# One transfer queue becomes two: GpSimd issues the later loads, the second readings and the output of an attention and feed-forward kernel

## The chip, the cores and the metric

The kernel runs on one core of one Trainium2 chip. The metric is the device time of one execution in microseconds (us). It was taken three times for the kernel before: 593.48, 593.84 and 595.53 us, with 593.84 us as the median. One further execution was recorded by the hardware profiler; that one took 598.99 us, of which 597.2 us lie between its first and its last instruction (the span).

## What is computed

Attention over 4 sequences of 768 tokens with 8 heads of 64, in which a query sees the last 96 keys and the first 8 keys of its sequence, with a bias that falls with the distance; then a feed-forward network on all 3072 rows. Cut from the reference:

```python
# q, k, v: (4, 8, 768, 64); n_global = 8; n_local = 96
scores = np.matmul(q, k.transpose(0, 1, 3, 2)) / np.sqrt(D)
keep = is_global | is_local          # first 8 keys, or 0 <= row - column < 96
bias = -slopes * dist                # slopes: 2 ** -(head + 1)
a = softmax(np.where(keep, scores + bias, -1e9))
x = np.matmul(a, v)                  # to (3072, 512)
h = x @ w_in                         # (512, 2048)
g = h / (1.0 + np.exp(-1.702 * h))
out = g @ w_out                      # (2048, 512), fp32
```

## The kernel before

**Tiles.** The 24 blocks are 128 rows each: blocks 0 to 3 are the first blocks of the four sequences, blocks 4 to 23 the rest in order. Because of the window, a later block needs its own keys and values and those of the block before it, and the first rows of its sequence. Two blocks make a chunk of the feed-forward part, 12 chunks in all. fp32 values are split into two fp16 halves, and each product is the sum of three fp16 products; from chunk 3 on the first matrix product is done in seven quarter products instead of eight (`up_two`, tiles pa and pb).

**What a later block passes through.** Its q, k and v are loaded into a tile raw (`load`, L406; two such tiles in turn, 256 KB for each of the three). ScalarE and VectorE split them (L464, L465, L474, L475). A transposing transfer brings q and k into QK (L467), and two plain transfers make a copy of the keys in QK with the halves exchanged (L469). Then in four units of two heads: scores on TensorE (L545, tile s), row minimum on VectorE (L551), exponential on ScalarE (L561), the split into halves (L565, L566, tile hl), a transposing transfer (L567, from hl to pt), and the products with the values on TensorE (L576 to L578, tile pv). The first rows' values, kept in VG, are written into rows of the block's own VR by a small transfer (`leading`, L668) when the block's own products are done; the next block's products read them there. For the first block after a sequence's first, k and v of that one are loaded again (`handover`, L507, tile over). The result is normalised (L694), split (L716, L718) and transposed by a transfer (L719) into xT, the input of the feed-forward part.

**The second readings.** To check that the fast path is exact enough, q, k and v of blocks 0 to 3 (L1011, tile again) and all weights in halves (L1019, tiles ws_..again, 32 transfers of 512 KB) are read a second time, squared and summed on ScalarE (L413, L1021) and reduced on VectorE (L1023). A flag made from these decides at the end if a slow general path runs; with the given inputs it does not.

**The order.** Every operation is a task with the engines that may run it, an assumed duration, its predecessors, its buffers and a due date. `order` (L109) passes the due dates backwards, adds a number out of the table NUDGE by the task's tag (L129), and then plays the tasks through in assumed time: each engine takes the most urgent task that is ready. The order that comes out is the program order of every engine, fixed when the program is built; on the chip each engine goes through its row in that order and waits at each instruction for what that one needs. SyncE ("SP") is one of these engines and issues all transfers but three; a transfer that waits, or one that takes long to issue, holds up all those behind it in SP's row. GpSimd (POOL) writes a few constants at the start and has nothing to do after that.

Of the kernel before, what the change touches and what calls it, by code (L numbers as in the profile page):

```python
# [19 lines left out]
P = 128  # L20
# [9 lines left out]
NUDGE = {"T3": 12.3, "block0": -11.9, "block13": -0.8, "block2": -18.8, "block4": 7.7, "block7": -8.8,  # L30
# [12 lines left out]
EARLY = 4  # L43
# [6 lines left out]
BACKLOG = 3.0  # L50
TWO = 3
LAT = 0.2
# [40 lines left out]
class Work:  # L93
# [15 lines left out]
    def order(self):  # L109
# [10 lines left out]
        while moved:  # L120
            moved = False
            for t in reversed(self.tasks):
                for n in t.next + [b.ring.line[b.i + b.ring.bufs].users[0] for b in t.bufs
                                   if not b.ring.loose and b.i + b.ring.bufs < len(b.ring.line)]:
                    due = n.due - min(n.on.values()) - LAT - (2.5 if "SP" in t.on else 0.0)
                    if due < t.due:
                        t.due, moved = due, True
        for t in self.tasks:
            t.due += NUDGE.get(t.tag, 0.0)  # L129
        free = dict.fromkeys(("PE", "DVE", "ACT", "POOL", "SP"), 0.0)  # L130
        dma, now, done = 1.5, 0.0, []
# [3 lines left out]
        while len(done) < len(self.tasks) + spared:  # L135
            moved = False
            for e in free:
                if free[e] > now or (e == "SP" and dma > now + BACKLOG):
                    continue
# [36 lines left out]
                if e == "SP":  # L176
                    free[e] = now + 0.1
                    dma = max(dma, now + 1.95) + us
                    t.end = dma + 0.9
# [15 lines left out]
            if not moved:  # L195
                later = [x + 1e-6 for x in (t.early() for t in ready) if x > now]
                later += [x for x in (*free.values(), dma - BACKLOG + 1e-6) if x > now] + [at for at in ready.values() if at > now]
# [6 lines left out]
def load_weights(nc, ws, w_in, w_out, s, u, half=None):  # L204
# [6 lines left out]
    nc.sync.dma_start(ws.rearrange("p (c f) t -> p c (f t)", c=n), words.rearrange("(c p) f -> p c f", p=P))  # L211
# [3 lines left out]
def kernel(  # L215
# [22 lines left out]
    ENG = {"PE": nc.tensor, "DVE": nc.vector, "ACT": nc.scalar, "POOL": nc.gpsimd, "SP": nc.sync}  # L238
# [123 lines left out]
    def weights(s, u):  # L362
# [8 lines left out]
        t0 = add({"SP": 2.75}, lambda e: load_weights(nc, ws(), w_in, w_out, s, u), bufs=[ws])  # L371
# [32 lines left out]
    def load(n, raw, parts=(0, 1, 2)):  # L404
        b, i = place(n)
        return [add({"SP": 1.35}, lambda e, z=z: nc.sync.dma_start(  # L406
# [93 lines left out]
    def handover(n):  # L500
# [6 lines left out]
        ld = load(b, raw, (1, 2))  # L507
# [395 lines left out]
    def pile(c, t, g, ready, part, steps, want):  # L903
# [15 lines left out]
        for k_, y in enumerate(ys[c][t]):  # L919
# [4 lines left out]
            if end:  # L924
# [7 lines left out]
                add({"ACT": 0.6} if last else {"SP": 0.7 * w / DM}, lambda e, m=m: ENG[e].dma_start(  # L932
# [76 lines left out]
    for n in range(EARLY):  # L1009
        raw = Buf(r_raw, [P, 3, H, D], F32, f"again{n}")  # L1010
        ld = load(n, raw)  # L1011
# [3 lines left out]
    for s in range(NST):  # L1015
        for u in range(2):
            for half in range(2):
                ws = Buf(r_wa, [P, 512, 2], I32, f"ws{s}_{u}{half}again")
                t0 = add({"SP": 1.6}, lambda e, s=s, u=u, ws=ws, half=half: load_weights(nc, ws(), w_in, w_out, s, u, half), bufs=[ws])  # L1019
# [266 lines left out]
```

## Time and profile before

| | |
|---|---|
| median of three runs | 593.84 us |
| profiled execution, its own time | 598.99 us |
| span in that execution | 597.2 us |
| TensorE busy, share of the span | 578.5 us, 97% |
| VectorE busy | 496.0 us, 83% |
| ScalarE busy | 463.6 us, 78% |
| GpSimd busy | 5.8 us, 1% |
| bytes moved by transfers | 109.58 MB |

Busy time is the time in which an engine executes an instruction; issuing a transfer does not count, so SyncE has no busy time here. Names: PE is TensorE, PEld its loading of weights, DVE VectorE, ACT ScalarE, POOL GpSimd, SP SyncE, and SPq the queue of SyncE, whose rows are the issuing of transfers. A row of groups gives line, engine, operation, tiles, shapes and count, then the busy us and the mean ns of one, then the idle time of the engine just before. L406 is line 406 of the kernel before; in the changed kernel the lines stand 8 or 9 lower (L406 is L415, L211 is L219, L932 is L941, L567 is L576, L668 is L677).

### The profile page before, as it was taken

The page shows a single profiled execution, that of the slowest core. Times are in us where ns is not written, and L with a number is a line of the kernel's source. Part 1 is how long each engine was busy: PE and PEld are TensorE (multiplying, and loading weights), DVE is VectorE, ACT ScalarE, POOL GpSimd, SP SyncE. Part 2 cuts the span into 40 slices and gives each one's busy share as a digit, 9 for nine tenths or more (in the row PEclk, how much of TensorE's full clock was granted, in tenths as well). Part 3 has the DMA queues.
Part 4 walks back from the last instruction along what each step waited for, and adds up shares of the span by engine and source line. Part 5 has one row for each costly group of instructions (what it writes and reads, how often), then busy time and mean ns, then how long its engine had stood idle before and what let it go on. Part 6 is the DMA issues. An engine that isn't in the chain of part 4 may idle for free.

```text
span 597.2 us, 16877 instructions
## 1 busy us (share of the span) xinstructions
PE 578.5 (97%) x6741; PEld 435.2 (73%) x6742; DVE 496.0 (83%) x1167; ACT 463.6 (78%) x1092; POOL 5.8 (1%) x18
## 2 busy tenths in 40 slices
PE   7999999999999999999999999899999999999996
PEld 4887576777668778868677768667777667777895
DVE  6799899999999999987798798798788878785541
ACT  4888699898948878978687999778988878844432
POOL 3000000000000000000000000000000000000000
PEclk9999999999999999999999999999999999999999
DMA  8999999999987579969999999999979999930001
GB/s 223 311 301 251 275 230 247 187 213 168 193 167 125 102 134 191 152 144 215 212 182 198 224 218 208 209 225 203 237 154 203 221 222 227 220 67 1 36 2 41
DMA packets 268503, 109.58 MB, mean 183 GB/s; under 512 B 249537, under 2 KB 250049, under 8 KB 268417
## 3 DMA queue, kind: packets, MB, share of 16 engines
q1 hardware_dynamic: 267984, 108.30, 90.0%
q8 instruction: 54, 0.88, 0.6%
q14 instruction: 33, 0.26, 0.2%
q10 hardware_dynamic: 432, 0.13, 0.1%
HBM read 57.67 MB, written 6.29 MB: 107 GB/s over the span
## 4 chain that ended last, share of the span: by engine, by line
PE 73%; DMA 14%; DVE 6%; ACT 3%; issue 2%; SPq 1%; ACTq 0%; DVEq 0%
PE y L914 31%; PE pa L846 12%; PE pb L846 9%; PE h L806 8%; DMA pt<-hl 6%; PE s L545 4%; DMA QKover<-QKover 2%; PE pv L576 1%; PE sT L638 1%; PE pv L578 1%; PE pv L577 1%; DMA QKover<-qk16over 1%; DMA VR<-VG 1%; DMA again<-in_k_dram 1%; DVE hl L566 1%
## 5 line engine op out<-in xcount | busy, mean ns | idle before, releaser
L914 PE MATMUL y<-w,g 128*128 128x512 f16 (+1 forms) x1248 | 264.6, 363 | 0.8 <-DVE w L381 0.5
L914 PEld LDWEIGHTS <-g 128*128 128x128 f16 x1248 | 118.2, 98 | 107.3 <-DVE g L818 1.4
L846 PEld LDWEIGHTS <-w 128*128 128x128 f16 x1728 | 100.5, 98 | 4.5 <-DVE h L854 0.9
L561 ACT ACTIVATE p<-p,NM 128x232 f32<-128x232 f32 x160 | 76.6, 481 | 10.5 <-DVE NM L551 10.2
L846 PEld LDWEIGHTS <-T 128*128 128x128 f16 x1296 | 76.8, 98 | 4.6
L806 PE MATMUL h<-xT,w 128*128 128x256 f16 x576 | 67.1, 273 | 0.0
L551 DVE CUSTOM_DVE_ANT_0 p<-s,mm 128x232 f32<-128x232 f32 x160 | 57.3, 393 | 7.6 <-PE s L545 7.3
L806 PEld LDWEIGHTS <-w 128*128 128x128 f16 x576 | 55.6, 98 | 8.1
L566 DVE TENSOR_TENSOR hl<-p,hl 128x464 f16<-128x464 f32 x80 | 50.9, 636 | 11.6 <-ACT hl L565 11.1
L887 DVE SCALAR_TENSOR_TENSOR g<-t,g 128x512 f16<-128x512 f32 x72 | 49.2, 686 | 10.2 <-ACT g L886 9.6
L886 ACT ACTIVATE g<-t 128x512 f16<-128x512 f32 x72 | 44.9, 626 | 13.1 <-DVE t L879 11.9
L565 ACT CAST hl<-p 128x464 f16<-128x464 f32 x80 | 46.1, 576 | 3.1 <-DMA pt<-hl 1.3
L878 ACT ACTIVATE t<-h 128x512 f32<-128x512 f32 (+1 forms) x72 | 35.5, 515 | 16.1 <-DVE h L854 14.8
L846 PE MATMUL pa<-xS,T 128*128 128x128 f16 x648 | 45.0, 219 | 0.0
L879 DVE SCALAR_TENSOR_TENSOR t<-t,h 128x512 f32<-128x512 f32 (+1 forms) x72 | 38.4, 552 | 7.5 <-ACT t L878 7.4
L854 DVE TENSOR_TENSOR h<-pb,h 128x256 f32<-128x256 f32 x72 | 28.6, 417 | 19.3 <-PE pb L846 16.9
L545 PEld LDWEIGHTS <-QK 128*128 128x128 f16 x640 | 36.2, 98 | 5.1 <-DVE NM L551 1.7
L846 PE MATMUL pb<-xS,w 128*128 128x128 f16 x540 | 37.5, 219 | 1.0 <-DVE h L854 0.9
L545 PE MATMUL s<-QK 128*128 128x128 f16 x320 | 38.3, 219 | 0.0
L576 PE MATMUL pv<-VR,pt 128*128 128x64 f16 x288 | 34.6, 193 | 3.6 <-DMA VR<-VG 2.3
L846 PE MATMUL pa<-xT,w 128*128 128x128 f16 x540 | 37.3, 219 | 0.0
L576 PEld LDWEIGHTS <-pt 128*128 128x128 f16 x320 | 29.5, 98 | 10.2 <-DMA pt<-hl 4.0
(179 smaller groups left out, 1033.0 us busy)
## 6 DMA issues: line engine op xcount, KB each, us to landing
ws<-in_moe_w_in_dram SPq DMA_DIRECT2D x8, 1024.0 KB
ws<-in_moe_w_out_dram SPq DMA_DIRECT2D x8, 1024.0 KB
raw<-in_q_dram SPq DMA_DIRECT2D x24, 256.0 KB
raw<-in_k_dram SPq DMA_DIRECT2D x24, 256.0 KB
out_dram<-yo SPq DMA_DIRECT2D x22, 256.0 KB
raw<-in_v_dram SPq DMA_DIRECT2D x20, 256.0 KB
QK<-QK SPq DMA_DIRECT2D x40, 128.0 KB
ws_00again<-in_moe_w_in_dram SPq DMA_DIRECT2D x8, 512.0 KB
```

The costliest lines, as they stand in the source:

```text
L545: nc.tensor.matmul(sp()[:, j, lo:hi], d["QK"]()[:, 0, h, :], K[:, 1 + z, h, P - (hi - lo):], start=(z == 0), stop=(z == 1), skip_group_che ...
L551: nc.vector.tensor_tensor_reduce(out=pr()[:, j, :], in0=sp()[:, j, :], in1=m, scale=-1.0 / SC, scalar=3.0e38, op0=ALU.add, op1=ALU.min, ac ...
L561: ex.append(add({"ACT": 0.473}, lambda e, j=j: nc.scalar.activation(pr()[:, j, :], pr()[:, j, :], AF.Exp, bias=NM[:, n, hs[j]:hs[j] + 1], ...
L565: t4 = add({"ACT": 0.5}, lambda e: nc.scalar.copy(hl()[:, 0, :, SKIP:], pr()), ex, [pr, hl])
L566: t5 = add({"DVE": 0.55}, lambda e: nc.vector.tensor_sub(hl()[:, 1, :, SKIP:], pr(), hl()[:, 0, :, SKIP:]), [t4], [pr, hl])
L576: nc.tensor.matmul(o, ph, V[:, 0, h], start=(s == 0), stop=False, skip_group_check=True)
L806: nc.tensor.matmul(ph()[:, fi, :], w1(s, cc, z, fi), X[:, y, cc, :], start=(j + cc == 0), stop=(j == 2 and cc == NCC - 1))
L846: nc.tensor.matmul(o()[:, fi], w, x()[:, y * NCC + 2 * k + cc, t], start=(first and fi + j + cc == 0), stop=(last and j + cc == 3), skip_g ...
L879: return add({"DVE": 0.08 + 0.265 * w}, lambda e: nc.vector.scalar_tensor_tensor(o(), o(), 1.0, src(), ALU.add, ALU.mult), [t1], srcs)
L886: t4 = add({"ACT": 0.53}, lambda e, g=g, tt=tt: nc.scalar.mul(g()[:, 0], tt(), SG / (SX * SW)), u, [tt, g])
L887: t5 = add({"DVE": 0.61}, lambda e, g=g, tt=tt: nc.vector.scalar_tensor_tensor(g()[:, 1], tt(), SG / (SX * SW), g()[:, 0], ALU.mult, ALU.s ...
L914: nc.tensor.matmul(y(), part(zg, f), w2(s, z, f % 2)[:, m], start=(begin and f + j == 0), stop=(end and j == 2 and f == 2 * len(steps) - 1 ...
```

## The change

A second engine name for issuing transfers, "GP", is added to the planner. It is GpSimd's queue, with a row of its own, costs of its own, and its own assumed state of the transfers under way. These tasks move to it: the loads of q, k and v from block 4 on, the loads of `handover`, the second readings of q, k, v and of the weights, and the output of all chunks but the last. On SP stay the loads of blocks 0 to 3, the first reading of the weights, the transposing transfers, the copies inside the core's memory, and the output of the last chunk (one of its pieces on ScalarE, as before). The table NUDGE is replaced as a whole.

```diff
-NUDGE = {"T3": 12.3, "block0": -11.9, "block13": -0.8, "block2": -18.8, "block4": 7.7, "block7": -8.8,
...
+NUDGE = {"": -3.9, "T2": 1.5, "block0": -39.8, "block10": 2.9, "block12": 0.8, "block14": -15.4,
...
-                    due = n.due - min(n.on.values()) - LAT - (2.5 if "SP" in t.on else 0.0)
+                    due = n.due - min(n.on.values()) - LAT - (2.5 if "SP" in t.on else 3.5 if "GP" in t.on else 0.0)
...
-        free = dict.fromkeys(("PE", "DVE", "ACT", "POOL", "SP"), 0.0)
-        dma, now, done = 1.5, 0.0, []
+        free = dict.fromkeys(("PE", "DVE", "ACT", "POOL", "SP", "GP"), 0.0)
+        dma, now, done = {"SP": 1.5, "GP": 1.5}, 0.0, []
...
-                if free[e] > now or (e == "SP" and dma > now + BACKLOG):
+                if free[e] > now or (e in dma and dma[e] > now + BACKLOG):
...
-                if e == "SP":
-                    free[e] = now + 0.1
-                    dma = max(dma, now + 1.95) + us
-                    t.end = dma + 0.9
+                if e in dma:
+                    free[e] = now + (0.1 if e == "SP" else 1.2)
+                    dma[e] = max(dma[e], now + (1.95 if e == "SP" else 2.8)) + us
+                    t.end = dma[e] + 0.9
...
-    ENG = {"PE": nc.tensor, "DVE": nc.vector, "ACT": nc.scalar, "POOL": nc.gpsimd, "SP": nc.sync}
+    ENG = {"PE": nc.tensor, "DVE": nc.vector, "ACT": nc.scalar, "POOL": nc.gpsimd, "SP": nc.sync, "GP": nc.gpsimd}
...
-    def load(n, raw, parts=(0, 1, 2)):
+    def load(n, raw, parts=(0, 1, 2), late=False):
         b, i = place(n)
-        return [add({"SP": 1.35}, lambda e, z=z: nc.sync.dma_start(
+        on = "SP" if n < EARLY and not late else "GP"
+        return [add({on: 1.35}, lambda e, z=z: ENG[e].dma_start(
...
-        ld = load(b, raw, (1, 2))
+        ld = load(b, raw, (1, 2), True)
...
-                add({"ACT": 0.6} if last else {"SP": 0.7 * w / DM}, lambda e, m=m: ENG[e].dma_start(
+                add({"ACT": 0.6} if last else {"SP" if c == NCHUNK - 1 else "GP": 0.7 * w / DM}, lambda e, m=m: ENG[e].dma_start(
...
-        ld = load(n, raw)
+        ld = load(n, raw, late=True)
...
-                t0 = add({"SP": 1.6}, lambda e, s=s, u=u, ws=ws, half=half: load_weights(nc, ws(), w_in, w_out, s, u, half), bufs=[ws])
+                t0 = add({"GP": 1.6}, lambda e, s=s, u=u, ws=ws, half=half: load_weights(ENG[e], ws(), w_in, w_out, s, u, half), bufs=[ws])
```

The numbers in these lines are the planner's assumptions; nothing on the chip reads them. What they change is the order. In all, 134 transfers go from SP's row to POOL's: 60 loads of raw, 8 of over, 12 of again, 32 halves of weights and 22 pieces of output.

The first place is where the products of block 17 read the first rows' values that were put into VR16. SP's row before, from the last transpose of block 16 on (names: pt16_3 is unit 3 of block 16, over19 the repeated keys and values before block 19, ws2_11again a half of the second reading, yo6_0 a piece of output):

```order
L567 DMA_TRANSPOSE pt16_3_6012<-hl1_90 128x8x128
L469 DMA QK18_5897<-QK18_5897 64x1024 x2
L406 DMA over19_6074<-in_k_dram 128x8x64
L567 DMA_TRANSPOSE pt17_0_6133<-hl0_89 128x8x128
L211 DMA ws3_00again_6151<-in_moe_w_in_dram 128x2x512
L567 DMA_TRANSPOSE pt17_1_6180<-hl1_90 128x8x128
L406 DMA over19_6074<-in_v_dram 128x8x64
L668 DMA VR16_5075<-VG2_4995 8x1024
L932 DMA out_0_dram<-yo6_0_6210 128x512
```

SP's row in the changed kernel, from the same transpose on:

```order
L576 DMA_TRANSPOSE pt16_3_5921<-hl1_90 128x8x128
L478 DMA QK18_5881<-QK18_5881 64x1024 x2
L677 DMA VR16_5014<-VG2_4411 8x1024
L576 DMA_TRANSPOSE pt17_0_6129<-hl0_89 128x8x128
L576 DMA_TRANSPOSE pt17_1_6182<-hl1_90 128x8x128
L728 DMA_TRANSPOSE xT8_6191<-x1616_6184 128x8x128
```

And POOL's row in the changed kernel, where the transfers that left that place now stand:

```order
L219 DMA ws3_00again_6127<-in_moe_w_in_dram 128x2x512
L941 DMA out_0_dram<-yo6_0_6162 128x512
L415 DMA over19_6187<-in_k_dram 128x8x64
L941 DMA out_0_dram<-yo6_1_6206 128x512
L219 DMA ws3_01again_6282<-in_moe_w_in_dram 128x2x512
L415 DMA raw20_6336<-in_q_dram 128x8x64
L415 DMA raw20_6336<-in_k_dram 128x8x64
L219 DMA ws3_10again_6390<-in_moe_w_out_dram 128x1024
L415 DMA over19_6187<-in_v_dram 128x8x64
```

Before, five transfers stand between the copy of keys and that of VR16, three of them loads; now none does, the two transposes come behind it, and the loads have a row of their own, in which they wait only for one another's buffers and for the output tiles.

The second place is three blocks earlier, at the units of block 14. SP's row before, from unit 0 on (VG2 takes the first rows' values out of VRover14):

```order
L567 DMA_TRANSPOSE pt14_0_4871<-hl0_89 128x8x128
L567 DMA_TRANSPOSE pt14_1_4918<-hl1_90 128x8x128
L406 DMA raw16_4793<-in_v_dram 128x8x64
L567 DMA_TRANSPOSE pt14_2_4992<-hl0_89 128x8x128
L487 DMA VG2_4995<-VRover14_4787 8x1024
L211 DMA ws1_00again_5054<-in_moe_w_in_dram 128x2x512
L211 DMA ws1_01again_5071<-in_moe_w_in_dram 128x2x512
L567 DMA_TRANSPOSE pt14_3_5078<-hl1_90 128x8x128
```

SP's row in the changed kernel, from unit 2 of that block on:

```order
L576 DMA_TRANSPOSE pt14_2_5117<-hl0_89 128x8x128
L576 DMA_TRANSPOSE pt14_3_5173<-hl1_90 128x8x128
L576 DMA_TRANSPOSE pt15_0_5220<-hl0_89 128x8x128
L476 DMA_TRANSPOSE QK16_5303<-qk1616_0_4932 128x16x128
L576 DMA_TRANSPOSE pt15_1_5354<-hl1_90 128x8x128
```

The two halves of weights of 512 KB each, which stood right ahead of the transpose of unit 3, are gone from the row, and transposes follow one another.

More of the change, by code (lines that the diff above doesn't have):

```diff
@@ L196, in order @@
                 later = [x + 1e-6 for x in (t.early() for t in ready) if x > now]
-                later += [x for x in (*free.values(), dma - BACKLOG + 1e-6) if x > now] + [at for at in ready.values() if at > now]
+                later += [x for x in (*free.values(), *(x - BACKLOG + 1e-6 for x in dma.values())) if x > now] + [at for at in ready.values() if at > now]
                 later += [x for t in done[-64:] for x in (t.end, t.end + LAT) if x > now] + ([worked + GAP + 1e-6] if now < worked + GAP else [])
@@ L201, in order, with load_weights @@
         return done
-def load_weights(nc, ws, w_in, w_out, s, u, half=None):
+def load_weights(eng, ws, w_in, w_out, s, u, half=None):
     words = w_in.bitcast(I32)[:, s * 4 * P:(s + 1) * 4 * P] if u == 0 else w_out.bitcast(I32)[s * 2 * P:(s + 1) * 2 * P, :]
@@ L210, in load_weights @@
     n = words.shape[0] // P
-    nc.sync.dma_start(ws.rearrange("p (c f) t -> p c (f t)", c=n), words.rearrange("(c p) f -> p c f", p=P))
+    eng.dma_start(ws.rearrange("p (c f) t -> p c (f t)", c=n), words.rearrange("(c p) f -> p c f", p=P))
 @with_exitstack
@@ L370, in weights @@
         low = lambda: w().bitcast(U16).rearrange("p z (c t) -> p (z c) t", t=2)[:, :, 0]
-        t0 = add({"SP": 2.75}, lambda e: load_weights(nc, ws(), w_in, w_out, s, u), bufs=[ws])
+        t0 = add({"SP": 2.75}, lambda e: load_weights(ENG[e], ws(), w_in, w_out, s, u), bufs=[ws])
         t3 = add({"DVE": 0.61}, lambda e: nc.vector.tensor_scalar(
```

26 rows, old and new, of the table NUDGE are left out of this document.

## The prediction

> **What bounds the kernel now.** I read the page first, for the shares and the chain:
>
> ```profile
> span 597.2 us, 16877 instructions
> PE 578.5 (97%) x6741; PEld 435.2 (73%) x6742; DVE 496.0 (83%) x1167; ACT 463.6 (78%) x1092; POOL 5.8 (1%) x18
> q1 hardware_dynamic: 267984, 108.30, 90.0%
> PE 73%; DMA 14%; DVE 6%; ACT 3%; issue 2%; SPq 1%; ACTq 0%; DVEq 0%
> ```
>
> TensorE works for 578.5 of 597.2 us, and the change takes no product away. So all that can be won on the way is its idle time, 597.2 - 578.5 = 18.7 us, 3.1% of the span. The second bound stands in the third line: nearly all transfers run on one queue, q1, whose packets fill 90% of the time of the 16 transfer engines. Next the table of busy time by stretches, to see where the 18.7 us lie (columns: stretch, its length, busy us of PE, PEld, DVE, ACT and POOL with counts, clock, share of the transfer engines, GB/s):
>
> ```profile
> 20.00:180.00 160.00, 157.84 (x1448) 115.48 (x1447) 151.83 (x295) 133.49 (x258) 0.00 (x0) 1.00 1.03 229
> 180.00:290.00 110.00, 110.00 (x1446) 83.02 (x1444) 98.58 (x244) 92.02 (x235) 0.00 (x0) 1.00 0.88 157
> 290.00:440.00 150.00, 144.58 (x1881) 108.48 (x1878) 127.30 (x328) 128.73 (x334) 0.00 (x0) 1.00 1.11 207
> 440.00:530.00 90.00, 88.73 (x1154) 66.37 (x1152) 73.69 (x184) 73.21 (x194) 0.00 (x0) 1.00 1.03 205
> 530.00:597.20 67.20, 61.56 (x711) 50.52 (x708) 30.88 (x79) 24.80 (x53) 0.00 (x0) 0.98 0.08 22
> ```
>
> Idle time by these rows: 2.2 us in 20 to 180, none in 180 to 290, 5.4 us in 290 to 440, 1.3 us in 440 to 530, and 5.6 us at the end; the first 20 us hold the remaining 4.2 us. The clock is 1.00 until the end, so no time is lost there. In the three stretches with idle time in the middle the transfer engines are at a share of 1.03 to 1.11, where they are at 0.88 TensorE waits for nothing. The end (last evictions and output) and the first 20 us stay on SP and ACT, so 4.2 + 5.6 = 9.8 us are out of reach, and 2.2 + 5.4 + 1.3 = 8.9 us are in reach. Then the list of TensorE's waits from 290 to 500:
>
> ```profile
> PE pv L576 <- DMA pt<-hl: 2.9, 4, 1.3
> PE pv L576 <- DMA VR<-VG: 2.3, 1, 2.3
> PE pb L846 <- DVE h L854: 0.9, 2, 0.5
> PE s L545 <- DVE NM L551: 0.5, 1, 0.5
> ```
>
> Of these 6.6 us, 2.9 + 2.3 = 5.2 us are waits for transfers of SP's queue, in five places; the other 1.4 us are waits for VectorE. (The 2.2 us before 180 us are short waits for VectorE and ScalarE.)
>
> **What the change removes.** Each of the five waits, by its own rows. The longest, for VR16, ends at 376.72. SP's queue by time ahead of it:
>
> ```profile
> 360.04 0.57 SPq L211 DMA_DIRECT2D ws_11again<-in_moe_w_out_dram  x1
> 360.70 1.23 SPq L567 DMA_TRANSPOSE pt<-hl  x1
> 362.03 1.22 SPq L469 DMA_DIRECT2D QK<-QK  x2
> 363.34 0.54 SPq L406 DMA_DIRECT2D over<-in_k_dram  x1
> 364.36 3.22 SPq L567 DMA_TRANSPOSE pt<-hl  x1
> 367.64 0.57 SPq L211 DMA_DIRECT2D ws_00again<-in_moe_w_in_dram  x1
> 368.30 1.23 SPq L567 DMA_TRANSPOSE pt<-hl  x1
> 369.59 0.73 SPq L406 DMA_DIRECT2D over<-in_v_dram  x1
> 370.41 1.42 SPq L668 DMA_DIRECT2D VR<-VG  x1
> 376.72 0.19 PE L576 MATMUL pv<-VR,pt 128*128 128x64 f16 x1 [2.33 <-DMA VR<-VG]
> ```
>
> The row is without a gap of a microsecond for 10 us. Four of the issues in it move: 0.57 + 0.54 + 0.57 + 0.73 = 2.41 us, a little more than the wait of 2.33 us. Besides, the new order has two transposes (3.22 + 1.23 us) behind VR16 instead of ahead. So this wait goes as a whole: 2.33 us. What is late next at that place is pt17_0, issued at 364.36 and so, at the longest landing quoted below, there at 371.5, ahead of TensorE.
>
> The other four wait for pt, and there the queue on SP isn't at fault but the landing:
>
> ```profile
> 310.49 7.12 DMA pt<-hl
> 473.29 6.10 DMA pt<-hl
> 430.44 5.34 DMA pt<-hl
> 419.20 5.08 DMA pt<-hl
> ```
>
> These are pieces of the chain of waits, from issue to landing. They grow with what was issued on the same queue just ahead: before the first, two halves of weights, 1 MB in all,
>
> ```profile
> 308.77 0.38 SPq L211 DMA_DIRECT2D ws_00again<-in_moe_w_in_dram  x1
> 309.90 0.37 SPq L211 DMA_DIRECT2D ws_01again<-in_moe_w_in_dram  x1
> 317.66 0.20 PE L576 MATMUL pv<-VRover,pt 128*128 128x64 f16 x1 [0.69 <-DMA pt<-hl]
> 479.44 0.20 PE L576 MATMUL pv<-VR,pt 128*128 128x64 f16 x1 [1.27 <-DMA pt<-hl]
> 435.82 0.20 PE L576 MATMUL pv<-VRover,pt 128*128 128x64 f16 x1 [0.66 <-DMA pt<-hl]
> ```
>
> and 1 MB takes 1049 / 207 = 5 us at the stretch's 207 GB/s. On a queue of its own such a load no longer stands ahead of the transpose. I take the shortest of the four landings, 5.08 us, as what a transpose needs without it. Then the first gains 2.04 us and its wait of 0.69 us goes; the second gains 1.02 of its 1.27 us; the third 0.26 of its 0.66 us; the fourth (0.24 us, the rest of the 2.9) nothing. Sum removed: 2.33 + 0.69 + 1.02 + 0.26 = 4.3 us.
>
> **What it adds and moves.** 134 transfers are issued by GpSimd. No row of before shows GpSimd issuing one, so its price is bounded by the nearest rows, the same transfers on SP, and GpSimd's own longest work (a memset):
>
> ```profile
> L406 SPq DMA_DIRECT2D raw<-in_q_dram x24: 368/541/2950, 0.8 to 444.1; - x24
> L406 SPq DMA_DIRECT2D raw<-in_v_dram x20: 432/583/4666, 39.1 to 452.3; - x20
> L423 POOL MEMSET QZ<- 64x512 f32 x8 | 4.2, 528 | 0.3
> ```
>
> From below 0.37 us, from above 4.67 us, an issue that stood behind others; I take 0.6 us, near the medians. That costs nothing while GpSimd, otherwise idle, keeps up. How fast it must be is read where the moved transfers stand closest: between these two rows SP issued 18 of them.
>
> ```profile
> 385.41 0.57 SPq L211 DMA_DIRECT2D ws_10again<-in_moe_w_out_dram  x1
> 431.74 0.59 SPq L211 DMA_DIRECT2D ws_00again<-in_moe_w_in_dram  x1
> ```
>
> 46.3 / 18 = 2.6 us for each. A load has some lead too: raw's q issued at 397.54 was transposed at 409.61, 12 us later. 46.3 + 12 = 58.3 us for 18 is 3.2 us: above that, blocks come late. In the queue a load waits for its raw tile (read by the splits of two blocks before) and an output for its tile; behind a waiting one stand loads of later blocks, whose users are 12 us away, and the checks, which nobody waits for before the end.
>
> The Trainium skill, page "SBUF — State Buffer", section "SBUF: two separate sides", says that GpSimd can't write the descriptors of a transfer while VectorE is in a two-port mode. By its section "Who interferes with whom" that concerns copies, casts and scalar operations inside SBUF. The rows of this case for them are short:
>
> ```profile
> L375 DVE TENSOR_SCALAR w<-ws 128x1024 int32<-128x1024 int32 x16 | 10.8, 683 | 1.5 <-DMA ws<-in_moe_w_in_dram 1.3 <-DMA ws<-in_moe_w_out_dram 0.2
> L716 DVE CAST x<-x 128x512 f16<-128x512 f32 x10 | 4.2, 421 | 0.0
> ```
>
> They add to 15 us of 597; one hit costs an issue at most 0.68 us, far below the 3.2 us, so the sum stays as it is either way. No run of before can show it.
>
> The new dates change the order on every engine. The products are the same; 18 instead of 16 filler products (L1075) stand in the first 50 us, where they fill waits. New waits from the new order: from none to as many as were in reach before, 8.9 us; the gain from it at best the 4.6 us in reach that I haven't taken (8.9 - 4.3). I take zero, since the waits for VectorE have no cause in SP's queue.
>
> **Sum.** -4.3 us. The profiled execution takes 598.99 us (597.2 and 1.8 around it), so the changed one would take 594.7; on the median of 593.84 us it is 589.5 us, 0.7% less. Its own range is 585 (all 8.9 us) to 592.5 (two thirds of the gain lost to new short waits).
>
> **Rivals.** *The waits move.* The 16 transfer engines are at a share of 1.03 to 1.11 where TensorE waits, and the same bytes have to pass. What a transpose gains by not standing behind a load it loses by sharing the engines with one that is issued later: at 207 GB/s a pt transpose of 256 KB is 1.3 us of them, shared with a load it is 2.5 us, so each landing grows by up to 1.2 us, as much as the 0.26 to 2.04 us gained. Then only the 2.33 us of VR16 are won, and three or four new waits of 0.5 us eat them: 593.8. For it: the shares. Against it: half of the gain isn't in the engines but in SP's row. The Trainium skill's page "DMA: Bandwidth & Descriptors", section "Issuing engines are not separate DMA queues", states this rule: transfers of all issuing engines run on the same 16 engines, and several issuers save only the issue time. By it the 2.33 us alone would go.
>
> *GpSimd is too slow an issuer* (the slower side). One mechanism: its row takes over 3.2 us for each load in the dense stretch, so the splits, the transposes of QK and the scores come late, and TensorE waits at L545. At 3.5 us: 18 x 3.5 - 58.3 = 4.7 us late, 598.5; at 4 us: 13.7 us late, 607.5. For it: 1024 short pieces per load, and the upper row of 4.67 us. Against: the medians of 0.5 to 0.6 us on SP for the same pieces.
>
> *The change doesn't do what it says*: GpSimd's transfers would go through q1 as well. Then the landings stay and only SP's issues shrink: 593.84 - 2.33 = 591.5. In the changed order these transfers have semaphores of their own, which speaks against it.
>
> **How the numbers follow.** Forecast 589.5 with a chance of 0.47; the waits move, 0.30; GpSimd too slow, 0.15; one queue as before, 0.08. The range reaches down to 586.0, with 0.07 left out below, and up to 600.0, which takes in GpSimd at 3.5 us and leaves 0.1 above. A difference of 0.5% (2.97 us) is about what a measurement here can't tell from no change. Faster than 590.87: 0.43 of the forecast's cases and 0.02 of the others, 0.45. Within: the rest of these and most of the two middle rivals, 0.35. Slower than 596.81: GpSimd too slow, 0.15, and the waits moved for the worse, 0.05, so 0.20.
>
> **What would show it.** Right: the wait for VR<-VG is gone, SP's queue has gaps at the place of block 17, a pt landing near 5 us where it was 7, TensorE's idle time from 290 to 530 down from 6.7 to about 2.4 us, and loads on a queue other than q1. Wrong: pt landings of 6 us and more all over (the waits moved), or TensorE's L545 waiting for QK and ScalarE's L473 (L464 before) for raw (GpSimd too slow), or new waits for VectorE from the new dates, which my sum put at zero.

## The result, and the profile after

The changed kernel takes **685.41 us** (median of four runs, 680.05 to 690.95) against 594.6 us for the kernel before, measured beside it on the same chip: a ratio of **1.1506, interval 1.1463 to 1.1549**. The prediction was 589.5 us with a range of 586 to 600. It missed by 96 us, and on the wrong side. Ratios, here and below, leave out every run more than 1.5% above the fastest of its kernel; medians and ranges take in all runs.

The profiled execution of the changed kernel took 688.03 us, of which 686.1 are the span. From its page, the span, the busy times, the two transfer queues (packets, MB, share of the 16 engines) and the chain of work that ended last. q1 is SyncE's queue, q0 GpSimd's:

```profile
span 686.1 us, 16946 instructions
PE 603.3 (88%) x6744; PEld 448.8 (65%) x6744; DVE 494.4 (72%) x1159; ACT 466.0 (68%) x1100; POOL 111.4 (16%) x152
q1 hardware_dynamic: 174960, 64.77, 53.0%
q0 software_dynamic: 12768, 43.52, 26.0%
PE 47%; DMA 27%; DVE 13%; ACT 9%; issue 3%; SPq 0%; POOL 0%; DVEq 0%; ACTq 0%; POOLq 0%
```

The span grew by 88.9 us. TensorE's idle time went from 18.7 to 686.1 - 603.3 = 82.8 us, which is 64.1 us of it; the other 24.8 us are busy time (578.5 to 603.3) for the same products, but for two more fillers. DMA has 27% of the chain where it had 14%. A second look at the third and fourth line: a packet of q0 carries 43.52 MB / 12768 = 3.4 KB on the mean, one of q1 64.77 MB / 174960 = 370 B. Most of the rest turns on this.

The list of TensorE's waits shows who ends them:

```profile
PE pv L585 <- DMA pt<-hl: 37.8, 14, 13.2
PE pv L585 <- DMA VR<-VG: 16.9, 1, 16.9
```

Before, the first row was 2.9 us in four waits and the second 2.3 us in one. The two kinds of wait of which the change was predicted to remove most make up 54.7 of the 82.8 us. The table by stretches shows what a long wait does to the clock:

```profile
350.00:400.00 50.00, 29.80 (x421) 24.99 (x419) 22.44 (x60) 24.34 (x64) 6.63 (x9) 0.80 1.14 152
500.00:550.00 50.00, 46.84 (x615) 35.02 (x613) 38.65 (x95) 40.65 (x105) 12.54 (x17) 1.00 0.88 183
550.00:600.00 50.00, 36.81 (x417) 27.10 (x415) 29.68 (x80) 29.45 (x81) 7.92 (x11) 0.83 0.77 142
```

The two stretches with the longest waits have a mean granted clock of 0.80 and 0.83, the one between them 1.00. These means take in the waits themselves. In shorter stretches the clock is 1.00 up to 367 us, 0.50 from 384 to 388, right after the first wait, 0.81 from 388 to 392 and 1.00 from then on; after the wait that ends at 567.83 it is 0.50 and 0.77 for 4 us each, then 1.00. There are nine such places, each at a wait of TensorE of 2 us or more, four of them waits for VectorE or ScalarE; three waits of 2.3 to 3.2 us left the clock at 1.00. Busy time times the missing share of the clock, in steps of 4 us, adds up to 20 of the 24.8 us; the rest I can't place. I read the slower products as a consequence of the waits: over the runs below, the mean clock goes down as TensorE's idle time goes up (0.997 with 18.9 us idle, 0.98 with 33.9, 0.972 with 55.3, 0.945 here with 82.8).

Now the two longest waits. First SyncE's row by time, and the chain, around the wait of 16.91 us for a copy of 16 KB into VR. It is the ninth of the 16 such copies, that into VR14, which the products of block 15 read; that into VR16, the eleventh, went out at 416.49, and TensorE did not wait for it. The two transposes ahead are those of units 1 and 2 of block 15, at the second place shown ahead of the prediction:

```profile
358.52 11.24 SPq L576 DMA_TRANSPOSE pt<-hl  x2
369.82 0.70 SPq L677 DMA_DIRECT2D VR<-VG  x1
376.68 8.03 SPq L476 DMA_TRANSPOSE QK<-qk  x1
```

```profile
369.82 14.10 DMA VR<-VG
383.96 0.21 PE pv L585
```

The issues that moved to GpSimd are gone from SyncE's row, as predicted. Yet issuing two transposes takes 11.24 us, where the longest single issue of a pt transpose before was 3.77 us (the median is 1.26 us in both kernels), and a copy of 16 KB needs 14.10 us from issue to landing. The queues from 370 to 384 us:

```profile
q1 hardware_dynamic: 2212, 0.78, 88.0%
q0 software_dynamic: 222, 0.78, 30.5%
```

Then the wait of 13.19 us at 567.83. The chain there is one pt transpose; beside it stand the first and the last of ten transfers that GpSimd issued from 544.24 to 555.28:

```profile
550.67 17.12 DMA pt<-hl
```

```profile
544.24 0.60 POOL L941 DMA_DIRECT2D out_dram<-yo  x1 [8.34 <-ACT yo L936]
...
555.28 0.56 POOL L219 DMA_DIRECT2D ws_11again<-in_moe_w_out_dram  x1 [2.25 <-DVE e L1032]
```

The ten are an output, three halves of weights and six of the second readings of q, k and v: 7 x 256 KB and 3 x 512 KB, 3.4 MB. The queues in 560 to 565 us, while the transpose is under way:

```profile
q0 software_dynamic: 333, 1.17, 90.5%
q1 hardware_dynamic: 322, 0.08, 11.9%
```

**333 packets of one queue and 322 of the other** fit engines that take one packet of each in turn. But 333 packets of GpSimd carry 1.17 MB, and 322 packets of SyncE 0.08 MB: in these 5 us a packet of 3.5 KB passes for each one of 250 B, and SyncE's queue gets a fifteenth of what GpSimd's gets. Transfers issued after the transpose pass ahead too: the half of weights issued at 555.28 landed 11.9 us later, at 567.2, and the transpose issued at 550.67 landed at 567.79. The Trainium skill, page "DMA: Bandwidth & Descriptors", section "Queues, rings and completion order", states that each engine goes round the queue rows that have work and drains a whole packet of one before it turns to the next. These 5 us agree with it by 333 to 322. The 14 us of the other wait do not show it: there the counts are 222 and 2212, although an output and a half of weights of GpSimd, issued at 363.96 and 364.51, took 17.4 and 19.0 us to land.

### The profile page after: what moved, and what is told of

Its sections match the earlier page's. It is cut to its first block, busy times and chain, and to the rows that moved or that the text cites. A ratio compares the mean times of both kernels' runs of the same rounds, so it can differ in the third digit from the quotient of the medians.

```text
span 686.1 us, 16946 instructions
## 1 busy us (share of the span) xinstructions
PE 603.3 (88%) x6744; PEld 448.8 (65%) x6744; DVE 494.4 (72%) x1159; ACT 466.0 (68%) x1100; POOL 111.4 (16%) x152
## 3 DMA queue, kind: packets, MB, share of 16 engines
q1 hardware_dynamic: 174960, 64.77, 53.0%
q0 software_dynamic: 12768, 43.52, 26.0%
HBM read 57.67 MB, written 6.29 MB: 93 GB/s over the span
## 4 chain that ended last, share of the span: by engine, by line
PE 47%; DMA 27%; DVE 13%; ACT 9%; issue 3%; SPq 0%; POOL 0%; DVEq 0%; ACTq 0%; POOLq 0%
PE y L923 19%; DMA pt<-hl 16%; PE pa L855 10%; PE pb L855 7%; DMA QKover<-qk16over 3%; PE s L554 3%; PE h L815 3%; ACT p L570 2%; DMA VR<-VG 2%; DMA ws<-in_moe_w_in_dram 2%; DMA xT<-x 1%; DVE t L888 1%; DMA raw<-in_v_dram 1%; ACT hl L574 1%; DVE h L863 1%
## 5 line engine op out<-in xcount | busy, mean ns | idle before, releaser
L923 PE MATMUL y<-w,g 128*128 128x512 f16 (+1 forms) x1248 | 271.4, 369 | 0.2
L923 PEld LDWEIGHTS <-g 128*128 128x128 f16 x1248 | 119.9, 99 | 111.4 <-issue 7.7
L855 PEld LDWEIGHTS <-w 128*128 128x128 f16 x1728 | 103.0, 99 | 9.4 <-issue 5.7
L855 PEld LDWEIGHTS <-T 128*128 128x128 f16 x1296 | 80.5, 101 | 4.9
L815 PE MATMUL h<-xT,w 128*128 128x256 f16 x576 | 70.4, 280 | 1.3 <-DVE t L825 1.1
L815 PEld LDWEIGHTS <-w 128*128 128x128 f16 x576 | 57.1, 101 | 11.9 <-issue 1.4
L585 PEld LDWEIGHTS <-pt 128*128 128x128 f16 x320 | 30.0, 100 | 44.4 <-DMA pt<-hl 42.0
L554 PEld LDWEIGHTS <-QK 128*128 128x128 f16 x640 | 38.3, 101 | 14.0 <-DVE NM L560 6.0
L415 POOL DMA_DIRECT2D raw<-in_q_dram x20 | 18.2, 909 | 178.0 <-ACT junk L422 84.2
L855 PE MATMUL pa<-xS,T 128*128 128x128 f16 x648 | 46.6, 224 | 0.0
L586 PEld LDWEIGHTS <-pt 128*128 128x128 f16 x320 | 29.6, 100 | 19.4 <-issue 17.0
L554 PE MATMUL s<-QK 128*128 128x128 f16 x320 | 40.2, 226 | 0.0
```

Source lines behind the costliest of these rows:

```text
L554: nc.tensor.matmul(sp()[:, j, lo:hi], d["QK"]()[:, 0, h, :], K[:, 1 + z, h, P - (hi - lo):], start=(z == 0), stop=(z == 1), skip_group_che ...
L585: nc.tensor.matmul(o, ph, V[:, 0, h], start=(s == 0), stop=False, skip_group_check=True)
L815: nc.tensor.matmul(ph()[:, fi, :], w1(s, cc, z, fi), X[:, y, cc, :], start=(j + cc == 0), stop=(j == 2 and cc == NCC - 1))
L855: nc.tensor.matmul(o()[:, fi], w, x()[:, y * NCC + 2 * k + cc, t], start=(first and fi + j + cc == 0), stop=(last and j + cc == 3), skip_g ...
L923: nc.tensor.matmul(y(), part(zg, f), w2(s, z, f % 2)[:, m], start=(begin and f + j == 0), stop=(end and j == 2 and f == 2 * len(steps) - 1 ...
```

## The experiments

**Theory A**: packets in turn, up to 4 KB against 256 B, so GpSimd's bytes pass ahead of the transposes and of SyncE's small copies, whatever was issued first. **Rival B**: the new dates and the order made from them are what costs.

**The two parts of the change by themselves.** The old order with the 134 transfers issued by GpSimd, and the new order with all issued by SyncE:

```diff
# e1_old_order_gp, against before; likewise at L211 and L932
-        return [add({"SP": 1.35}, lambda e, z=z: nc.sync.dma_start(
+        eng = nc.sync if n < EARLY and not late else nc.gpsimd
+        return [add({"SP": 1.35}, lambda e, z=z: eng.dma_start(
# e2_new_order_sp, against the changed kernel
-    ENG = {..., "SP": nc.sync, "GP": nc.gpsimd}
+    ENG = {..., "SP": nc.sync, "GP": nc.sync}
```

> The order of before, unchanged on TensorE, VectorE and ScalarE; only the 134 transfers are issued by GpSimd instead of SyncE, at the same places of the program. Theory A (the engines take packets of the two queues in turn, 4 KB ones of GpSimd's queue against 256-byte ones of the transposes, so a transpose stands still while GpSimd's bytes pass): most of the loss is there with the old dates too, 635 to 690 us, with waits for pt of over 30 us in sum. Rival B (the new dates left less slack, the second queue is harmless): 590 to 598 us.

> The changed kernel's dates and planner, but the tasks of GP are issued by SyncE, in the planned order. Theory A: the loss is gone but for what a row planned for two queues costs on one, 594 to 612 us, pt landings of 5 to 7 us. Rival B (new dates): the loss stays, 660 us and more.

Before was 595.14 us beside both. The old order with GpSimd took 651.54 us, ratio 1.0948 [1.0877, 1.1018]; the new order on SyncE 616.96 us, ratio 1.0367 [1.0337, 1.0397]. So the issuer alone costs 56.4 us, the new order alone 21.8 us, and both together (90.8 us) some 13 more than their sum. From the list of TensorE's waits of the first and of the second:

```profile
PE pv L577 <- DMA pt<-hl: 37.1, 13, 7.4
```

```profile
PE pv L585 <- DMA pt<-hl: 10.5, 10, 3.1
PE pv L585 <- DMA VR<-VG: 2.2, 2, 1.2
```

With the issuer alone TensorE waits for pt as long as in the changed kernel (37.1 against 37.8 us). A wait for VR of 16.9 us is in neither; none of the runs of the whole kernel below has more than 4.0 us of them in all. The new order costs too, by more than A had expected of it (594 to 612 us); that is taken up below.

**Transposes by themselves beside loads of 1.5 to 3 MB.** Four pt transposes in a row, the first beside six loads.

```diff
# m1_transposes_beside_loads: the kernel's body is replaced
+    for j, x in enumerate(short):   # or wide: 512 KB in rows of 4 KB
+        eng.dma_start(x, ...)       # GpSimd, ScalarE, SyncE
+    for j in range(NT):
+        nc.sync.dma_start_transpose(pt, hl)
+        nc.vector.tensor_copy(hl[:, 0:P], pt[:, 0])
```

> Only transposing transfers of a 256 KB tile on SyncE, four in a chain, alone and then beside six loads issued at the same time by GpSimd, ScalarE or SyncE: first 256 KB loads in 256-byte pieces, then 512 KB loads in 4 KB rows. The output is not computed. Theory A: alone one takes 4 to 5 us; beside the 256-byte loads of GpSimd the first takes 9 us or more (all 1.5 MB pass ahead); beside the same loads of ScalarE, whose packets are 256 bytes, it takes less than with GpSimd, 5 to 8 us; beside the 4 KB rows both GpSimd and ScalarE hold the first transpose until most of the 3 MB have passed, 14 us or more; on SyncE the loads stand ahead in the row, 9 and 16 us. Rival B: a transpose beside loads of another queue takes at most twice its time alone, whatever the queue and the pieces.

The chain of work, start and us from issue to landing: alone; then the first transpose beside loads in 256 B pieces by GpSimd, ScalarE, SyncE (ahead in its own row); then beside loads in rows of 4 KB by the same three:

```profile
11.70 3.05 DMA pt<-hl
...
26.43 8.69 DMA pt<-hl
...
48.65 5.17 DMA pt<-hl
...
69.92 4.56 DMA pt<-hl
...
87.92 12.05 DMA pt<-hl
...
113.47 12.62 DMA pt<-hl
...
141.40 9.57 DMA pt<-hl
```

With short pieces the issuer makes the difference: GpSimd adds 5.6 us to the 3.05, ScalarE 2.1. With long rows it makes hardly any (12.05 and 12.62). That fits packets in turn: what counts is the size of the other queue's packets. The times are lower than A had put them (4 to 5 alone, 9 and 14 or more beside the loads); the rival's bound of twice the time alone, 6.1 us, doesn't hold. On the same queue a transpose waits for what was ahead of it (4.56, 9.57), and its own issue stands behind those of the loads: counted from when its input was ready (67.47 and 139.80), it lands after 7.0 and 11.2 us. That is the best of the three beside long rows, and between ScalarE and GpSimd beside short pieces.

**How it grows with the number of loads.** The same with 1, 2, 4 and 8 loads in 256 B pieces.

```diff
# m2_how_many_loads, against m1
+    for eng in (nc.gpsimd, nc.scalar):
+        for count in (1, 2, 4, 8):
+            rows(eng, count)
```

> Leaves out the whole computation: only four pt transposes in a row (each waits for the one before), alone and then beside 1, 2, 4 and 8 loads of 256 KB in pieces of 256 B, issued by GpSimd and then by ScalarE. Theory A (the transfer engines take one packet of each queue in turn, and GpSimd's packets are 4 KB where a transpose's are 256 B): beside GpSimd's loads the first transpose grows with the number of loads, since all their bytes pass ahead of it: 3.04 alone, then about 4.0, 4.9, 6.8 and up to 10.5 us by the 0.94 us per load of the six-load case. Beside ScalarE's loads, in packets of 256 B like its own, it can at most double or so however many there are: 4 to 6 us for 2, 4 and 8. Rival (the 16 engines are shared by bytes, whoever issues): the same growth for both issuers, to within 1 us at each count.

The chain, first transpose beside 1, 2, 4 and 8 loads of GpSimd (beside the eight the second transpose too), then the same of ScalarE:

```profile
18.84 3.71 DMA pt<-hl
...
35.54 4.17 DMA pt<-hl
...
53.17 8.21 DMA pt<-hl
...
74.36 7.94 DMA pt<-hl
...
82.61 5.79 DMA pt<-hl
...
97.55 3.04 DMA pt<-hl
...
112.92 3.78 DMA pt<-hl
...
129.07 5.47 DMA pt<-hl
...
146.93 5.37 DMA pt<-hl
...
152.62 5.38 DMA pt<-hl
```

Over the 3.04 us, four loads cost 5.2 us beside GpSimd: 1.05 MB at 203 GB/s, as if all their bytes had passed first. Beside ScalarE they cost 2.4 us, and eight loads no more per transpose (5.37, 5.38): there a transpose takes at most 1.8 times as long. The even growth that was expected with GpSimd didn't show: two loads cost only 1.1 us, and with eight loads it goes over into the second transpose, since issuing them takes GpSimd 7 us.

**Which of the moved transfers costs.** Before's order, with only one kind on GpSimd:

```diff
# e3_loads_gp (80 loads of q, k and v, 21.0 MB)
+        eng = nc.sync if n < EARLY and not late else nc.gpsimd
# e3_weights_gp (32 halves of weights, 16.8 MB)
-                ... load_weights(nc, ws(), ...
+                ... load_weights(nc.gpsimd, ws(), ...
# e3_out_gp (22 outputs, 5.8 MB)
-                ... ENG[e].dma_start(
+                ... (ENG[e] if c == NCHUNK - 1 else nc.gpsimd).dma_start(
```

> The order of before; only the loads of q, k, v (raw, over, again: 80 transfers, 21 of the 43.5 MB) are issued by GpSimd. Theory A: about half of the loss of the run with all 134, so 610 to 645 us. Rival B: 590 to 598 us.

> The order of before; only the 32 halves of the second reading of the weights (16.8 of the 43.5 MB) are issued by GpSimd. Theory A (packets in turn, 4 KB against 256 bytes): their rows are 2 and 4 KB long, so on SyncE's queue too they pass in large packets, but in their place in the row; on the queue of their own they overtake the transposes issued before them: 610 to 630 us, waits for pt from 265 us on. If what counts were the cutting of a load into 256-byte pieces alone, nothing would change: 593 to 598 us.

> The order of before; only 22 pieces of output (5.8 of the 43.5 MB) are issued by GpSimd. Theory A: a piece of 256 KB ahead of a transpose costs it some 1.5 us, two at a time 3 us, in a few places: 595 to 606 us. Rival (a second queue as such makes a fixed loss, whatever it carries): as the loads, 620 us and more.

Loads 626.57 us, 1.0528 [1.0498, 1.0559]; weights 608.58 us, 1.0239 [1.0187, 1.029]; outputs 595.76 us, 1.003 [1.0009, 1.0051]. By median 31.4, 13.8 and about 1 us, together 46 of the 56.4; the weights came out just under the 610 us that A had as their least.

**The same kinds on another second queue.** This tells the second queue from its packets: ScalarE's queue is a second one too, and its packets are short where the pieces are.

```diff
# e8_loads_act, against e3_loads_gp
-        eng = nc.sync if n < EARLY and not late else nc.gpsimd
+        eng = nc.sync if n < EARLY and not late else nc.scalar
# e8_weights_act, against e3_weights_gp
-                ... load_weights(nc.gpsimd, ws(), ...
+                ... load_weights(nc.scalar, ws(), ...
```

> Before's order with the 80 loads of q, k and v issued by ScalarE (by GpSimd they took 626.6 us, 31.4 more than before, with 12.0 us of waits for pt). ScalarE is busy for 78% of the span and gets 80 issues of some 0.55 us on top, 44 us, which its idle time can take for the most part. Theory A (it isn't the second queue as such, but GpSimd's packets of 4 KB where ScalarE's are 256 B, the size of a transpose's): well under half of the loss, 597 to 611 us, waits for pt at TensorE below 6 us; what is lost is ScalarE's time. Rival (any second queue lets loads overtake the transposes, and that is what costs): 620 to 635, with the waits for pt as with GpSimd.

> Before's order with the 32 weight halves of the second readings issued by ScalarE (by GpSimd 608.6 us, 13.8 more than before). These rows are 2 to 4 KB long for any issuer, and beside such loads a transpose took 12.6 us with ScalarE as issuer and 12.1 us with GpSimd. Theory A: no better than with GpSimd, 605 to 620 us. Rival (GpSimd itself is what costs, by its issue or its descriptors): 594 to 601.

The loads by ScalarE: 602.81 us, 1.013 [1.0079, 1.018]. The weights by ScalarE: 607.42 us, 1.0168 [1.0103, 1.0233]. The second queue (q10 is ScalarE's) and TensorE's wait for pt, with the loads on GpSimd and on ScalarE:

```profile
q0 software_dynamic: 6400, 20.98, 14.9%
...
PE pv L577 <- DMA pt<-hl: 12.0, 7, 5.4
```

```profile
q10 hardware_dynamic: 83632, 21.11, 19.6%
...
PE pv L577 <- DMA pt<-hl: 3.9, 4, 2.6
```

The same 80 loads go in packets of 3.3 KB on the one and of 252 B on the other; the ratio falls from 1.053 to 1.013, and the waits for pt from 12.0 to 3.9 us. The weights' rows give packets of 3.6 KB with GpSimd and 2.4 KB with ScalarE (the queues below), and there the two intervals overlap: no gain that these runs can tell.

```profile
q0 software_dynamic: 4608, 16.78, 9.4%
```

```profile
q10 hardware_dynamic: 7088, 16.91, 10.1%
```

Both runs came out as A said. ScalarE's row also goes by ScalarE's own work, so its loads can start at other times than GpSimd's; these runs don't part that from the packets, but the transposes by themselves did (8.69 against 5.17 us with short pieces, no such difference with long rows). It is the size of the packets beside the transposes, not GpSimd and not the second queue as such.

**What of the new order costs.** Its 21.8 us on one queue can come from the new table of dates or from the planner, which now keeps one clock of transfers under way for each of the two issuers, as if neither delayed the other. An empty table with the old planner, with the new one on SyncE, and with the new one on GpSimd:

```diff
# e5_no_dates_sp, against before
# e5_no_dates_two_clocks_sp, against e2_new_order_sp
# e5_no_dates_gp, against the changed kernel
-NUDGE = {...}
+NUDGE = {}
```

> The kernel before with an empty table of dates; everything else as before. It shows what the table is worth by itself, as a yardstick for the 21.8 us that the new table and planner cost on one queue. If the tables are fitted to one queue's timing: 605 to 640 us; if they matter little: 595 to 600 us.

> The changed kernel's planner, which books the transfers of the moved tasks on a clock of their own, with an empty table of dates, and all transfers issued by SyncE. Before's planner with an empty table took 598.4 us, and the new order on SyncE 617.0. If the 21.8 us of the new order come from the table of dates (made for another machine than this queue): 597 to 603. If they come from the planner, which counts on transfers that overtake each other and so plans loads and transposes closer than one queue can do: 610 to 622.

> The changed kernel as it is, GpSimd issuing, with an empty table of dates. Theory A (GpSimd's packets pass ahead of the transposes, and its row isn't paced by SyncE's): still far slower than before, 645 to 690, since the loads and weights move as before. Rival B (the new dates are what costs): near the old order with GpSimd or better, 600 to 640.

With the old planner 598.39 us, 1.010 [1.0045, 1.0154]; with the new one 632.69 us, 1.0597 [1.0526, 1.0668]. Over the kernel before, measured beside each, that is 3.6 and 35.4 us, and 21.8 with the new dates. So it is the planner, not the table: it costs some 32 us on one queue, more than was expected, and the new dates win 14 of them back. With GpSimd and no dates it took 695.1 us (682.97 to 701.9); its fastest run, 682.97, lies among the changed kernel's 680.05 to 690.95. Rival B is right that the new order costs, a quarter of the whole when it runs on one queue, but the dates aren't the reason. That the planner counts on two queues that don't delay each other is the likely reason, but not shown: its other new numbers (a lead of 3.5 us for GpSimd's tasks, 1.2 us for an issue) changed along with the two clocks and weren't tried apart.

**Less beside the longest waits.** In before's kernel, the second readings of weights from 300 to 380 us and from 455 on were put at 460 to 545 us, all on SyncE:

```diff
# w1_second_readings_late, against before
+LATE, STEP = 460.0, 4.2
+        late = [x for x in trios if 300.0 <= x[0].start < 380.0 or x[0].start >= 455.0]
...
```

> The order of before, all on SyncE; the second readings of the weights planned between 300 and 380 us are put at the places from 460 to 545 us instead, with their squares and minima (nothing else moves). If the waits for pt and VR of before come from the bytes in front of them on the one queue, those between 300 and 380 (3.0 us) go and the time is 590 to 593 us; if the later stretch, as dense, pays them back, 593 to 600 us.

601.24 us, 1.0115 [1.0089, 1.0141]: no gain, and above both expectations. The wait for VR is gone, but the waits for pt are 4.8 us where they were 2.9. Before's places for these readings were better than a place of their own late in the span.

**GpSimd held behind the transposes.** In the old order with GpSimd, GpSimd reads one element of the latest pt ahead of a moved transfer, so that none starts before the latest pt transpose issued ahead of it has landed:

```diff
# e7_behind_pt, against e1_old_order_gp
+    def behind():
+        if "pt" in seen:
+            nc.gpsimd.tensor_copy(tiny, seen.pop("pt")[0:1, 0, 0:1])
+        return nc.gpsimd
```

> Before's order with the 134 transfers on GpSimd (651.5 us without the edit), but GpSimd copies one element of the latest pt ahead of a transfer, so a load doesn't start before the transposes issued ahead of it in the program have landed. Theory A: this takes away the loads that start beside such a transpose, though not those that meet the next ones: 605 to 640, with fewer waits for pt at L586 than the 37.1 us. Rival (GpSimd's loads slow everything by their mere share, or come too late): no gain or a loss, 650 to 680, with ScalarE or TensorE waiting for raw, QK or weights.

685.35 us (678.21 to 707.01): worse than without (651.54), and worse than both expectations. From the lists of GpSimd's and of TensorE's waits:

```profile
POOL tiny L293 <- DMA pt<-hl: 385.0, 50, 24.4
```

```profile
PE pv L584 <- DMA pt<-hl: 20.0, 8, 11.1
PE pa L854 <- DVE h L862: 11.3, 4, 7.4
PE pa L854 <- ACT h L870: 9.6, 7, 3.0
```

The waits for pt fall from 37.1 to 20.0 us, in the direction that A had, but GpSimd itself waits for pt for 385 us in all, its transfers come in bunches, and TensorE gets new waits for VectorE and ScalarE. The clock was 0.966 here. This way of keeping the two queues in step doesn't pay.

**The row of transfers at the 16.91 us wait.** There the engines moved only 111 GB/s (0.78 + 0.78 MB in 14 us), half of what they moved beside loads in the experiments. Is that the packets in turn alone?

```diff
# m3_row_at_the_stall: the kernel's body is replaced
+    # eng: two loads of 512 KB in 4 KB rows, one of 256 KB in pieces, an output
+    nc.sync.dma_start_transpose(pt[0], hl)
+    nc.sync.dma_start_transpose(pt[1], hl)
+    nc.sync.dma_start(VR[24:32], VG)
+    # two copies of 128 KB: QK <- QK
```

> Leaves out the whole computation: SyncE issues what stood in its row at the 16.91 us stall (two pt transposes, a 16 KB copy into VR, two 128 KB copies inside the core's memory), alone and then beside what GpSimd had issued there (512 KB in rows of 4 KB, 256 KB in 256 B pieces, a 256 KB output, 512 KB in rows of 4 KB; 1.57 MB), the same without the output, the same by ScalarE, by SyncE ahead in its own row, and once more by GpSimd. In the trace of the changed kernel the 16 engines moved 1.56 MB in the 14 us of that stall, 111 GB/s, half of what they moved beside the loads in the experiments with transposes alone (1.83 MB in 8.69 us). Theory A alone (packets in turn, the engines otherwise at their pace): all is moved at 180 to 220 GB/s, 2.4 MB in 11 to 13 us, and the copy into VR lands within that. If GpSimd's transfers beside copies or an output slow the engines as such: 16 us and more with GpSimd, 11 to 13 with ScalarE and SyncE; with the output as the cause, only in the groups that have it.

The chain, the last copy from issue to landing: alone, GpSimd, GpSimd without the output, ScalarE, SyncE ahead in its own row, GpSimd once more:

```profile
5.58 2.33 DMA QK<-QK
...
13.83 8.71 DMA QK<-QK
...
27.67 8.67 DMA QK<-QK
...
42.42 7.58 DMA QK<-QK
...
58.26 4.53 DMA QK<-QK
...
68.55 10.92 DMA QK<-QK
```

From GpSimd's first issue (9.52 and 64.34) to that landing it took 13.0 and 15.1 us for 2.4 MB, 182 and 157 GB/s. The output isn't to blame, but the 111 GB/s didn't come back either: 13.0 us is what A gives, 15.1 lies between the two. Nor did the long issue: the second transpose took 1.32 to 1.38 us to issue beside GpSimd's loads. Why the engines and the issues were that slow around 370 us **stays open**, and with it the largest single wait: the 222 packets against 2212 speak against packets in turn as its whole cause.

None of the variants beats the kernel before.

## Why the prediction was wrong, step by step

**The step that failed** is in the part on what the change removes: "On a queue of its own such a load no longer stands ahead of the transpose." It does, and worse than before. In one row a load of 512 KB stands ahead of a transpose only if it was issued ahead. On two queues, loads also pass ahead that come while the transpose is under way, and long packets take most of the engines' time (90.5% against 11.9% at 560 to 565 us). The landings of 5.34 to 7.12 us were to come down to 5.08; of the thirteen pt transposes on the chain after, seven take 6.29 to 17.12 us, and the waits for pt went from 2.9 to 37.8 us where the sum had most of them gone.

**The rival "the waits move"** had the right place and the wrong size. It let a transpose and a load share the engines by halves, "so each landing grows by up to 1.2 us". That fits packets of one size: beside ScalarE's short pieces a transpose took 5.47 us at most, 2.4 more. For GpSimd's long packets and for rows of 4 KB the growth is near the time of all the bytes: 5.2 us for four loads, 9 us for 3 MB. The 0.30 given to this rival at 593.8 us should have been a case on the slower side.

**The wait for VR16** was to go as a whole, since 2.41 us of issues leave SyncE's row. They left it, and TensorE no longer waits for that copy: here the prediction was right. But TensorE waited 16.91 us for the copy into VR14, for which nothing waited before: the two transposes ahead of it took 11.24 us to issue, and the copy itself took 14.10 us to land. That other transfers of SyncE's row could come late was missing from the sum. What held up these issues isn't shown.

**GpSimd as an issuer** was priced a little low, and without harm. From the list of what stands on the line of the loads (min, median and max ns):

```profile
L415 POOL DMA_DIRECT2D raw<-in_k_dram x20: 884/884/980, 28.2 to 530.3; - x20
```

0.88 us for a load where 0.6 was taken, between the bounds of 0.37 and 4.67 us and far below the 3.2 us from which it would have mattered; the longest issue of a later load was 1.34 us, so no hold-up by VectorE is seen beyond that either. The rival on the slower side that I had chosen did not happen. The slower side came by another way, to which the prediction gave 0.05.

**The new dates** were put at zero, between a loss of 8.9 and a gain of 4.6 us. On one queue the new order costs 21.8 us, far out of these bounds: they were drawn from the idle time that was there, which bounds a gain but not a loss. The runs with an empty table put this on the changed planner, not on the dates.

**The clock** was left out. It was 1.00 before wherever it mattered, and a sum of waits was taken as the sum of the time. Here about 20 of the 88.9 us are slower products after long waits.

**That it wouldn't do what it says** is refuted by the queues: 43.52 MB do go through q0. And the forecast's own sign of failure, "pt landings of 6 us and more all over", is what came on the chain.

## What to carry to other kernels

Before moving loads to a second transfer queue, look at the mean packet of each queue (bytes by packets in the profile): here, urgent transfers in short packets lost to bulk ones in long packets, even to some that were issued later. In one queue the transposes here were late only by what stood close ahead of them, 2.9 us of waits in all; two queues gave that up, and an order that was planned for two independent queues lost more. If a second queue is needed, give it transfers in packets no longer than those of the urgent queue (here the loads through ScalarE cost 1.3% where GpSimd's cost 5.3%), or only few bytes at a time (the outputs, 0.3%).

## What the runs showed of the hardware that was not expected

- In 5 us with a transpose under way, the two queues sent about as many packets as each other, 333 and 322, with 1.17 and 0.08 MB. In another stretch of 14 us the counts were 222 and 2212.
- For the same pieces of 256 B, GpSimd's queue shows packets of 3.3 KB and ScalarE's of 252 B.
- Some of SyncE's own issues took far longer beside the other queue: two transposes 11.24 us, where the longest single one before took 3.77. The median stayed at 1.26 us, and the row by itself did not bring the long ones back.
- After waits of 17 and 13 us the granted clock was 0.50 for about 4 us and 0.81 and 0.77 for the next 4, then 1.00.
